# Memory attention with two gated layers on one core: the first layer's output products taken over pairs of batches, and the order around them rewritten

## Chip, core and metric

The kernel runs on one core of one Trainium2 chip. The metric is the device time of one execution in microseconds (us), the median of several runs.

## What is computed

The reference, cut to what matters. Batch 4, heads 8, sequence 576, head size 64, 32 memory slots; 2304 tokens of 512, hidden size 1536:

```python
a    = softmax(phi over the sequence)            # per batch, head and memory slot
k_m  = einsum('bhsm,bhsd->bhmd', a, k)
v_m  = einsum('bhsm,bhsd->bhmd', a, v)
attn = softmax(q @ k_m.T / 8) @ v_m              # over the 32 memory slots
x    = attn as 2304 x 512
x    = ((x @ w_a) * (x @ w_b)) @ w_out           # first layer
out  = (silu(x @ w_gate) * (x @ w_val)) @ w_out2 # second layer
```

The weights arrive as 8-byte floats and are decoded on the core to 4-byte ones.

## The kernel before

The program has two parts.

**The planned part** holds the attention and the first layer. Its order is written out by hand as a table (`PLAN`, L608 to L671 before): a row of names, each of which advances one generator by one step. Every engine runs its instructions in exactly the order in which the table issues them, and the DMA issues of SP stand in that order too. A second table, `STEPS`, says for some operations on which engine (A = ACT, V = DVE, P = POOL) they run.

The names that matter here. `p` (`att_phi`, L267) is the softmax of phi and the k_m, v_m products of one batch ("kv" products, 72 small ones), `q` transposes q, `s` makes the scores, `o` transposes the attention weights, `c` decodes a chunk of a weight, `W` loads one, `P K L Q` load phi, k and v, q. `z` (`warm`, L588) is a dummy product of the identity with itself, 256 columns wide, whose result nobody reads.

The first layer works transposed, and since x is attention weights times v_m, its input products go through v_m @ w. For a step f (128 of the 1536 hidden columns) and a batch b:

- `v` (`vw_part`, L472) makes v_m @ w for one step, for two batches from step 2 on: 8 products of 32 rows by 256 columns per batch ("vw" in the profile). ACT copies the high part (`vwh`, L500), DVE makes the low part (`vwl`, L502).
- `a` and `b` (`s1_a`, `s1_b`, L515 and L519) are the two input products of 12 matmuls each, 288 columns wide. After `b`, ACT copies it to `bs` (L523), DVE multiplies by `a` (L525), ACT makes the high part `gh` (L529) and DVE or POOL the low part `gl` (L531).
- `d` (`s2_part`, L537) is the output product of one batch, one of four 128-column blocks `dt` of the output, and two steps: two halves of 288 columns with 6 matmuls each, high and low parts crossed. It is added to `acc` by DVE (L570), or copied there for the first two steps (L568). With the last two steps, ACT and DVE split the sum into `xh` and `xl` (L580, L582), the input of the second layer.

All PE results go through four PSUM buffers (`bank2`). `g` tiles come from a pool of four, each for one batch and one step.

**The second part** (L714 on) is the second layer: units of `gate` and `val` products (24 matmuls of 384 columns, L738), their activation, and output products of 512 columns. A scheduler places it, behind the planned part on every engine.

Of the kernel before, what the change touches and what calls it, by code (L numbers as in the profile page):

```python
# [18 lines left out]
def kernel(  # L19
# [452 lines left out]
    def vw_part(parts):  # L472


        pv = bank2("vw").rearrange("c g (n x) -> c g n x", n=2)
        for n, (f, b) in enumerate(parts):
            for j in range(PR):
                for g in range(2):
                    rows = slice(D * g, D * g + D)
                    nc.tensor.matmul(  # L480
                        pv[M * j:M * j + M, g, n],
                        lhsT=vt[b][rows, M * j:M * j + M],
                        rhs=whl[f][0][rows, j].rearrange("p t c -> p (t c)"),
                        start=True,
                        stop=True,
                        tile_position=(D * g, M * j),
                    )
        yield
        f, b = parts[0]
        if f > 1 or b not in vw_2:  # L490
            vw_2[b] = [
                vw_p.tile([128, 2, 2, 256], FP32R, tag=f"vw{x}", name=f"vw{x}") for x in "hl"
            ]
        t = vw_2[b]
        o = int(f == 1)
        for n, (f, b) in enumerate(parts):
            vw_t[b, f] = [x[:, o + n] for x in t]
        n = len(parts)
        hi, lo = [x[:, o:o + n].rearrange("c n g x -> c g n x") for x in t]
        nc.scalar.copy(out=hi, in_=pv[:, :, 0:n])  # L500
# [36 lines left out]
    def s2_part(b, idx, dt):  # L537
        first, last = idx[0] == 0, idx[-1] == NF - 1
        if first and b not in acc:
            acc[b] = slot(f"acc{b}", [128, KD, 2, HB], FP32)  # L540
        if last:
            j = b // 2
# [5 lines left out]
            if dt not in x2[j][1]:  # L548
                x2[j][1][dt] = ph_p.tile(
                    [128, 2 * S], FP32R, tag=("phi", "sc")[dt // 2], name=f"xl{dt}"  # L550
                )
# [1 line left out]
        cs = slice(dt * 128, (dt + 1) * 128)
        for hb in range(2):
            terms = []
            for i in idx:
                gh, gl = g_t[b, i]
                oh, ol = ohl[i]
                terms += [
                    (oh[:, cs], gh[:, hb]),  # L560
                    (oh[:, cs], gl[:, hb]),
                    (ol[:, cs], gh[:, hb]),
                ]
            products(p[:, hb, 0:HB], terms)
# [2 lines left out]
        if first:
            copy(eng("acc", KD * b + dt), acc[b][:, dt], pv)  # L568
        else:
            nc.vector.tensor_tensor(  # L570
                out=acc[b][:, dt], in0=pv, in1=acc[b][:, dt], op=ALU.add
            )
        if last:
            yield
            cs = slice(b % 2 * S, (b % 2 + 1) * S)
            hi, lo = [
                x[:, cs].rearrange("p (h s) -> p h s", h=2)
                for x in (x2[j][0][:, dt], x2[j][1][dt])
            ]
# [2 lines left out]
            nc.vector.tensor_tensor(out=lo, in0=acc[b][:, dt], in1=f32(hi), op=ALU.subtract)  # L582

    vws = [((f, b),) for b in range(B) for f in range(2)] + [
        ((f + o, 2 * p), (f + o, 2 * p + 1))
        for f in range(2, NF, 2) for p in range(2) for o in range(2)
    ]
# [26 lines left out]
    c4 W8 c5 b0.0 p2 v1 v3 p2 c5 W9 c4 s1.0 b0.0 v3 v1 c4 p2 v1 s1.1 s1.0 b0.0 c13 s1.0 c13 b0.1
    L3 s1.1 s1.0 e2 s1.1 a0.1 s1.0 b0.1 s1.1 s1.1 p2 c13 b0.1 b0.1 b0.1 c7 p2 q2.1 p2 c7 c7
    d0.0.0 p2 q2.1 p2 d0.1.0 p3 d0.0.0 s1.1 s1.0 p3 p2 d0.1.0 c13 d0.3.0 p2 p3 s1.1 p2 s1.0 p3
    d0.3.0 d0.2.0 p3 c13 p3 o1.1 c7 W10 o1.0 q2.0 d0.2.0 e3 o1.1 p3 q2.0 o1.1 o1.0 c7 o1.0 c10
    p3 q2.2 W18 v5 p3 c10 c10 p3 c10 a1.1 q2.2 v5 p3 c10 v5 s2.1 c10 W14 p3 c10 s2.1 s2.0 p3
    s2.1 p3 s2.1 a1.0 s2.0 Q3 s2.1 s2.0 b1.1 s2.1 s2.0 s2.1 s2.0 b1.0 b1.1 b1.1 s2.0 v4 b1.1
# [233 lines left out]
```

## Time and profile before

| what | before |
|---|---|
| median of 3 runs | 868.36 us (867.11 to 868.68) |
| the profiled execution's own time | 867.69 us |
| span from first to last instruction | 865.9 us |
| PE busy | 839.0 us, 97% |
| DVE, ACT, POOL busy | 57%, 36%, 28% |
| mean granted clock of PE | 0.997 |

The profile is of one execution; 1.79 us of its time lie outside the span. PE is the matmul engine; its matmuls are pipelined, so that one lasts longer than the distance to the next one, and costs are read from the distance. In a profile L459 (tile `s`) is the line of all output products of both layers, L467 of the first layer's input products, L480 of vw, L591 of the dummies.

### The profile page before, as it was taken

How to read it: one execution, taken by the hardware profiler on the slowest of the kernel's cores; microseconds unless marked ns; L12 is line 12 of the kernel's file. 1: busy time of each engine (PE TensorE's matmuls, PEld its weight loads, DVE VectorE, ACT ScalarE, POOL GpSimd, SP SyncE). 2: the span in 40 equal slices, each digit the busy share in tenths (PEclk: the TensorE clock that was granted, in tenths of full speed). 3: DMA queues.
4: the chain of work that ended last, by engine and by line, in shares of the span. 5: the costliest groups of instructions: out<-in, count | busy, mean ns of one | idle time of the engine just before them, and what ended most of it. 6: DMA issues, size and time to landing. Idle time of an engine off the chain costs nothing.

```text
span 865.9 us, 15099 instructions
## 1 busy us (share of the span) xinstructions
PE 839.0 (97%) x6526; PEld 785.6 (91%) x6526; DVE 491.5 (57%) x671; ACT 315.2 (36%) x491; POOL 245.1 (28%) x183
## 2 busy tenths in 40 slices
PE   4798999999999999999999999999999999999997
PEld 3587999999999999999998999999889999998996
DVE  4887855757467577488554145535645453644334
ACT  3565746425344353265345333214212321410110
POOL 3662543435144153143133013204302220410000
PEclk9999999999999999999999999999999999999999
DMA  9974131302003012011211103102110200000015
GB/s 326 380 251 128 51 98 30 118 25 78 22 25 123 25 50 74 2 50 50 74 48 53 46 1 98 49 1 73 40 34 14 84 25 1 1 1 1 1 49 170
DMA packets 42434, 59.95 MB, mean 69 GB/s; under 512 B 4224, under 2 KB 30848, under 8 KB 42368
## 3 DMA queue, kind: packets, MB, share of 16 engines
q1 hardware_dynamic: 40928, 56.63, 20.3%
q10 hardware_dynamic: 1440, 2.36, 0.8%
q8 instruction: 51, 0.84, 0.4%
q14 instruction: 15, 0.12, 0.0%
HBM read 54.26 MB, written 4.72 MB: 68 GB/s over the span
## 4 chain that ended last, share of the span: by engine, by line
PE 91%; DVE 3%; DMA 2%; issue 1%; SPq 1%; ACT 1%; POOL 1%; POOLq 0%; DVEq 0%; ACTq 0%
PE s L459 34%; PE gate L738 17%; PE val L738 17%; PE s1a L467 9%; PE s1b L467 9%; PE vw L480 2%; DMA phi<-in_phi_dram 2%; PE sc L381 1%; PE warm L591 1%; DVE dec_a L173 1%; PE kv L303 1%; PE sc L391 0%; DVE dec_a L177 0%; DVE rm L263 0%; POOL dec_a L169 0%
## 5 line engine op out<-in xcount | busy, mean ns | idle before, releaser
L459 PE MATMUL s<-oh,g 128*128 128x512 f32 x432 | 137.0, 390 | 0.0
L459 PE MATMUL s<-gh,oh 128*128 128x288 f32 x384 | 114.9, 299 | 0.0
L459 PE MATMUL s<-gh,ol 128*128 128x288 f32 x384 | 113.2, 295 | 0.0
L459 PE MATMUL s<-gl,oh 128*128 128x288 f32 x384 | 113.1, 295 | 0.0
L189 POOL TENSOR_TENSOR dec_a<-dec_a,raw 128x512 int32<-128x512 int32 x48 | 65.7, 1369 | 119.2 <-DVE dec_a L177 53.0
L459 PEld LDWEIGHTS s<-oh,g 128*128 128x128 f32 x432 | 81.1, 188 | 16.4
L204 POOL TENSOR_TENSOR wl<-dec_a,wh 128x512 fp32r<-128x512 f32 x24 | 30.8, 1301 | 210.3 <-ACT wh L202 210.3
L459 PE MATMUL s<-ol,g 128*128 128x512 f32 x216 | 84.4, 391 | 0.0
L753 DVE TENSOR_TENSOR sg<-val,sg 128x768 f32<-128x768 f32 x36 | 34.5, 958 | 84.2 <-PE val L738 83.9
L750 DVE TENSOR_TENSOR sg<-gate,sg 128x768 f32<-128x768 f32 x36 | 34.4, 956 | 73.4 <-ACT sg L749 73.2
L783 DVE TENSOR_TENSOR oacc<-s,oacc 128x1024 f32<-128x1024 f32 (+1 forms) x50 | 55.8, 1115 | 35.6 <-PE s L459 34.7
L459 PEld LDWEIGHTS s<-gh,oh 128*128 128x128 f32 x384 | 72.2, 188 | 3.9 <-ACT bs L523 0.8
L738 PE MATMUL gate<-d_2x,wh 128*128 128x384 f32 x288 | 73.2, 335 | 0.0
L738 PE MATMUL gate<-d_2x,wl 128*128 128x384 f32 x288 | 73.2, 334 | 0.0
L738 PE MATMUL val<-d_2x,wl 128*128 128x384 f32 x288 | 73.2, 334 | 0.0
L738 PE MATMUL val<-d_2x,wh 128*128 128x384 f32 x288 | 73.1, 334 | 0.0
L459 PEld LDWEIGHTS s<-gh,ol 128*128 128x128 f32 x384 | 72.1, 188 | 0.0
L459 PEld LDWEIGHTS s<-gl,oh 128*128 128x128 f32 x384 | 72.0, 188 | 0.0
L165 ACT ACTIVATE raw<-raw 128x512 int32<-128x512 uint32 x72 | 48.0, 676 | 65.5 <-DMA raw<-in_moe_w_out_dram 48.6
L112 DVE TENSOR_TENSOR g<-sg,g 128x768 fp32r<-128x768 f32 (+1 forms) x48 | 45.2, 956 | 39.5 <-ACT g L111 39.5
L111 ACT CAST g<-sg 128x768 fp32r<-128x768 f32 (+1 forms) x48 | 31.0, 670 | 92.9 <-DVE sg L753 92.9
L177 DVE SCALAR_TENSOR_TENSOR dec_a<-raw,dec_a 128x512 int32<-128x512 int32 x72 | 56.4, 784 | 1.7
(131 smaller groups left out, 1753.9 us busy)
## 6 DMA issues: line engine op xcount, KB each, us to landing
raw<-in_moe_w_out_dram SPq DMA_DIRECT2D x24, 512.0 KB, 3.3
raw<-in_moe_w_b_dram SPq DMA_DIRECT2D x12, 512.0 KB, 4.4
raw<-in_moe_w_a_dram SPq DMA_DIRECT2D x12, 512.0 KB, 4.1
raw<-in_moe_w_val_dram SPq DMA_DIRECT2D x12, 512.0 KB, 3.5
raw<-in_moe_w_gate_dram SPq DMA_DIRECT2D x12, 512.0 KB, 4.1
d_0x<-in_k_dram SPq DMA_DIRECT2D x5, 576.0 KB, 10.3
d_0x<-in_v_dram SPq DMA_DIRECT2D x5, 576.0 KB, 10.7
phi<-in_phi_dram SPq DMA_DIRECT2D x4, 576.0 KB, 10.9
```

The source lines that it names most:

```text
L111: nc.scalar.copy(out=hi, in_=src)
L112: (eng or nc.vector).tensor_tensor(out=lo, in0=src, in1=f32(hi), op=ALU.subtract)
L165: nc.scalar.activation(out=lo, in_=lo.bitcast(U32), func=ACTF.Copy, scale=2.0 ** -29)
L177: nc.vector.scalar_tensor_tensor(out=a, in0=hi, scalar=-0x40000000, in1=a, op0=ALU.bitwise_and, op1=ALU.bitwise_or)
L189: nc.gpsimd.tensor_tensor(out=a, in0=a, in1=lo, op=ALU.add)
L204: nc.gpsimd.tensor_tensor(out=dst[1], in0=src, in1=f32(dst[0]), op=ALU.subtract)
L459: nc.tensor.matmul(dst, lhsT=l, rhs=r, start=(i == 0), stop=(i == n - 1))
L467: nc.tensor.matmul(p[:, hb, 0:HB], l, x, start=(i == 0), stop=(i == n - 1))
L738: nc.tensor.matmul(p[:, h, 0:CH], l[:, kt, o], r[:, c0:c0 + CH], start=(n == 0), stop=(n == 3 * KD - 1),)
L750: nc.vector.tensor_tensor(out=t, in0=pg, in1=t, op=ALU.mult)
L753: nc.vector.tensor_tensor(out=t, in0=pv, in1=t, op=ALU.mult)
L783: nc.vector.tensor_tensor(out=dst, in0=p[:, 0:n], in1=dst, op=ALU.add)
```

## The change

- Output products of the first layer from step 2 on run over a **pair of batches** (`f`, new `s2_part(j, n, f)`): g tiles are shared by two batches (1152 columns; the pool has two of them in place of four half as wide), and a unit is 384 columns of the pair for two of the four blocks `dt`, 12 matmuls. Steps 0 and 1 keep the old form (`s2_first`, 288 columns). `acc` of batches 0 and 1 is one tile; batches 2 and 3 use the tiles acc2 and acc3 by `dt`.
- `v` makes two steps for two batches **in one row** (two PSUM buffers, 32 small products).
- The table is new: the units of a kind stand together, the 13 dummies at its end are gone, and 15 stand in its first part where 4 stood.
- DVE, ACT and POOL steps are dealt out anew in `STEPS`; k and v of batch 0 are loaded ahead of the first weight chunk.

```diff
-    g_p = p1.enter_context(tc.tile_pool(name="g", bufs=4))
+    g_p = p1.enter_context(tc.tile_pool(name="g", bufs=2))
...
     def vw_part(parts):
-        pv = bank2("vw").rearrange("c g (n x) -> c g n x", n=2)
-        for n, (f, b) in enumerate(parts):
+        pvs = []
+        for part in parts:
+            pv = bank2("vw").rearrange("c g (n x) -> c g n x", n=2)
+            for n, (f, b) in enumerate(part):
...
+            pvs.append(pv)
         yield
+        for part, pv in zip(parts, pvs):
...
+            nc.scalar.copy(out=hi, in_=pv[:, :, 0:n])
+            yield
+            nc.vector.tensor_tensor(out=lo, in0=pv[:, :, 0:n], in1=f32(hi), op=ALU.subtract)
+            yield
...
+    def of_batch(x, n):
+        return x[:, n % 2 * S:(n % 2 + 1) * S].rearrange("p (h s) -> p h s", h=2)
...
-        g = [g_p.tile([128, 2, HB], FP32R, tag=f"g{x}", name=f"g{x}") for x in "hl"]
+        n, half = (b, f) if f < 2 else ((b // 2, f), b)
+        if n not in g_t:
+            g_t[n] = [g_p.tile([128, 2 * S], FP32R, tag=f"g{x}", name=f"g{x}") for x in "hl"]
+        g = [of_batch(x, half) for x in g_t[n]]
...
+    def s2_first(b, dt):
+        p = bank2("s2")
+        gs = [[of_batch(x, f) for x in g_t[b]] for f in range(2)]
+        products_halves(p, s2_terms(gs, range(2), dt))
+        yield
+        copy(eng("acc", KD * b + dt), of_batch(acc_of(b // 2, dt)[:, dt % 2], b), p[:, :, 0:HB])
+
+    def s2_part(j, n, f):
+        last = f + 2 == NF
+        cs = slice(n // 2 * CH, (n // 2 + 1) * CH)
+        dts = n % 2 * 2, n % 2 * 2 + 1
...
+        p = bank2("s2")
+        gs = [[x[:, cs] for x in g_t[j, i]] for i in (f, f + 1)]
+        for o, dt in enumerate(dts):
+            products(p[:, o, 0:CH], s2_terms(gs, (f, f + 1), dt))
+        yield
+        a = acc_of(j, dts[0])[:, :, cs]
+        nc.vector.tensor_tensor(out=a, in0=p[:, :, 0:CH], in1=a, op=ALU.add)
+        if last:
+            yield
+            nc.scalar.copy(out=x2[j][0][:, dts[0]:dts[0] + 2, cs], in_=a)
+            yield
+            for o, dt in enumerate(dts):
+                nc.vector.tensor_tensor(
+                    out=x2[j][1][dt][:, cs], in0=a[:, o], in1=f32(x2[j][0][:, dt, cs]),
+                    op=ALU.subtract,
+                )
...
     PLAN = """
-    P0 W1 K0 L0 W0 Q0 p0 P1 c1 W3 p0 c1 c1 p0 p0 K1 p0 c1 p0 c1 L1 e0 p0 c0 W2 c0 c0 c0 p0 c0 z0
...
-    d2.2.10 c39 d2.3.10 d3.2.10 c39 d3.2.10 d3.0.10 d2.3.10 d3.2.10 d2.3.10 z4 d3.3.10 z5
-    d3.0.10 z6 z7 d3.1.10 d3.0.10 z8 d2.3.10 z9 z10 d3.0.10 z11 z12 z13 z14 z15 z16
+    P0 L0 K0 W1 W0 Q0 p0 P1 W3 p0 p0 p0 K1 z0 p0 p0 z1 e0 L1 p0 c1 c1 c1 c1 c0 W2 c0 c0 c1 c0 p0
...
+    f1.5.10 f1.3.10 f1.5.10 f1.2.10 f1.2.10 f1.4.10 f1.3.10 f1.2.10 f1.3.10 f1.3.10
+    f1.4.10 f1.4.10 f1.4.10
```

Three places in PE's order. **The border between the two parts**, on PE. Before, the last unit of `d` is followed by the dummies and then by the second layer's first `gate`:

```order
L459 MATMUL s_4927<-gl,oh 128x288
L459 MATMUL s_4927<-gh,ol 128x288
L591 MATMUL warm<-ident 128x256 x13
L738 MATMUL gate<-d_2x,wh 128x384 x2
L738 MATMUL gate<-xl_4525,wh 128x384 x2
L738 MATMUL gate<-d_2x,wl 128x384 x2
```

With the change the last `f` unit (batches 2 and 3) stands directly ahead of the same `gate`:

```order
L459 MATMUL s_4624<-gl,oh 128x384
L459 MATMUL s_4624<-gh,ol 128x384
L762 MATMUL gate<-d_2x,wh 128x384 x2
L762 MATMUL gate<-xl_4295,wh 128x384 x2
L762 MATMUL gate<-d_2x,wl 128x384 x2
```

The dummies went; from `gate` on, PE's order of units is the same in both kernels.

**Ahead of an output product in the middle**, on PE. Before, v_m @ w of one step (two batches, vt_98 and vt_99) stands between other units:

```order
L459 MATMUL s_3257<-gl,oh 128x288
L459 MATMUL s_3257<-gh,ol 128x288
L480 MATMUL vw<-w,vt_98 32x256 x8
L480 MATMUL vw<-w,vt_99 32x256 x8
L459 MATMUL s_3293<-gh,oh 128x288
```

With the change two steps follow each other (four rows of vw), ahead of a unit of 384 columns:

```order
L467 MATMUL s1a<-d_1x,vwl 128x288 x2
L482 MATMUL vw<-w,vt_98 32x256 x8
L482 MATMUL vw<-w,vt_99 32x256 x8
L482 MATMUL vw<-w,vt_98 32x256 x8
L482 MATMUL vw<-w,vt_99 32x256 x8
L459 MATMUL s_1981<-gh,oh 128x384
```

Such rows of vw number 18 before from step 2 on (16 of one step, 2 of two) and 10 now; for steps 0 and 1 they are 7 before and 5 now.

**Behind the second batch's kv products**, in the start, on PE. Before:

```order
L363 MATMUL qT<-ident,d_0x 128x128 x8
L428 MATMUL aT<-ident,sc 128x128 x5
L338 MATMUL kvT<-ident,kvm 128x128 x3
L428 MATMUL aT<-ident,sc 128x128 x4
L363 MATMUL qT<-ident,d_0x 128x128 x8
L480 MATMUL vw<-w,vt_97 32x256 x8
L467 MATMUL s1a<-d_1x,vwh 128x288 x4
```

With the change:

```order
L619 MATMUL warm<-ident 128x256
L363 MATMUL qT<-ident,d_0x 128x128 x8
L428 MATMUL aT<-ident,sc 128x128 x5
L619 MATMUL warm<-ident 128x256
L338 MATMUL kvT<-ident,kvm 128x128 x3
L428 MATMUL aT<-ident,sc 128x128 x4
L363 MATMUL qT<-ident,d_0x 128x128 x2
L619 MATMUL warm<-ident 128x256 x2
L482 MATMUL vw<-w,vt_96 32x256 x8
L482 MATMUL vw<-w,vt_97 32x256 x16
L467 MATMUL s1b<-d_1x,vwh 128x288 x4
```

Dummies came in between, three rows of vw stand together, and the larger part of q's transposes (x8) moved behind.

## Rows read from the trace of the kernel before

**Rows 1.** The page: busy time, and the span in 40 slices.
```profile
PE 839.0 (97%) x6526; PEld 785.6 (91%) x6526; DVE 491.5 (57%) x671; ACT 315.2 (36%) x491; POOL 245.1 (28%) x183
...
PE   4798999999999999999999999999999999999997
```

**Rows 2.** Windows: us; busy of PE, PEld, DVE, ACT, POOL; granted clock; DMA share, GB/s.
```profile
0.00:22.00 22.00, 10.76 (x178) 8.55 (x178) 9.51 (x24) 8.40 (x13) 8.11 (x13) 1.00 0.96 327
22.00:90.00 68.00, 58.30 (x1051) 48.33 (x1052) 56.48 (x102) 40.91 (x75) 34.03 (x27) 0.97 0.70 240
90.00:412.72 322.72, 322.06 (x2925) 307.37 (x2923) 214.88 (x293) 145.38 (x227) 123.91 (x84) 1.00 0.17 55
412.72:866.00 453.28, 447.87 (x2377) 421.37 (x2375) 210.62 (x255) 120.56 (x179) 79.08 (x60) 1.00 0.14 41
```

**Rows 3.** The chain that ended last, in order of time: start us, us, what.
```profile
394.36 12.75 PE s L459 x96
407.11 5.61 PE warm L591 x26
412.72 4.18 PE gate L738 x24
...
458.51 5.48 PE s L459 x24
```

**Rows 4.** The chain between 200 and 232 us: rows of one and of two steps.
```profile
202.84 1.02 PE vw L480 x32
...
226.41 1.89 PE vw L480 x64
```

**Rows 5.** PE around one row of vw, in order of time.
```profile
381.68 0.29 PE L459 MATMUL s<-gh,ol 128*128 128x288 f32 x1
381.91 1.09 PE L480 MATMUL vw<-w,vt 64*32 64x256 f32 x32
```

**Rows 6.** From an s1a product to its g, by engine, in order of time.
```profile
384.34 0.43 PE L467 MATMUL s1a<-aT,vwl 128*128 128x288 f32 x2
...
384.81 0.76 DVE L525 TENSOR_TENSOR bs<-s1a,bs 128x576 f32<-128x576 f32 x1 [0.55 <-PE s1a L467]
...
385.61 0.68 ACT L529 CAST gh<-bs 128x576 fp32r<-128x576 f32 x1
...
386.36 1.43 POOL L531 TENSOR_TENSOR gl<-bs,gh 128x576 fp32r<-128x576 f32 x1 [0.29 <-ACT gh L529]
```

**Rows 7.** What PE waited for from 90 to 412 us: total, times, longest us.
```profile
PE s1b L467 <- DVE vwl L502: 0.7, 1, 0.7
```

**Rows 8.** DVE writing the last low parts of batches 0 and 1.
```profile
389.74 2.53 DVE L582 TENSOR_TENSOR xl<-d_0x,d_2x 128x576 fp32r<-128x576 f32 x2
```

**Rows 9.** Groups by line: the wide product of DVE with a PSUM operand.
```profile
L753 DVE TENSOR_TENSOR sg<-val,sg 128x768 f32<-128x768 f32 x36 | 34.5, 958 | 84.2 <-PE val L738 83.9
```

**Rows 10.** What PE waited for from 22 to 90 us (first of 12).
```profile
PE kv L303 <- issue: 2.8, 2, 1.8
```

**Rows 11.** Marks in PE's order in the start.
```profile
22.34 0.30 PE L275 MATMUL mx<-ident,pm 128*128 128x128 f32 x1 [0.80 <-DVE pm L265]
...
32.21 1.07 PE L363 MATMUL qT<-ident,d_0x 128*128 128x128 f32 x8 [0.51 <-DMA d_0x<-in_q_dram]
...
53.77 0.31 PE L303 MATMUL kv<-kv,phi 64*32 64x128 f32 x4
...
72.09 0.42 PE L363 MATMUL qT<-ident,q 128*128 128x128 f32 x2
```

**Rows 12.** The chain: half a score unit.
```profile
47.05 0.62 PE sc L381 x16
47.67 0.23 PE sc L391 x4
```

**Rows 13.** Windows of two stretches, columns as in rows 2.
```profile
69.00:72.00 3.00, 1.16 (x62) 0.69 (x45) 2.18 (x5) 1.60 (x3) 0.00 (x0) 1.00 0.59 175
73.00:76.50 3.50, 3.50 (x26) 3.19 (x20) 2.09 (x5) 1.72 (x5) 1.50 (x2) 0.51 0.00 0
```

More of the change, by code (lines that the diff above doesn't have):

```diff
@@ L443 @@
     STEPS = """
-    gl PPPVVPVVVPVPVPPPPPPVPVVPVVPPPVVVVVVVVVPVVVPPPVVP rmx VVVV mul PVVPVPVP sub VVVVVVVV sum
-    PPPV qT AAAVAAAAAVAA acc AAAAAAVAVVAAAAAA clamp VPVPVPPPVVVPVPPVPPVVVPVVVVVPPVVPVVPPPVPVPV
+    gl VPPVVPPPVVVPPVVVVVPPVVPVPVVVPVPPVVPVPPVVVPVPPPVV rmx VVVV mul PVPVPPPV sub VVVVVVVV sum
+    VPPV qT AAAVAVVAAAVV acc VVVAVAVAAVVVVVVA clamp VVVVVPVPPVVVPPPVVPVVPPVVVVVVVVVVPVVPVVPVVV
     """
@@ L472, in vw_part @@
     def vw_part(parts):
-        pv = bank2("vw").rearrange("c g (n x) -> c g n x", n=2)
-        for n, (f, b) in enumerate(parts):
[L477 to L487, printed above, removed]
@@ L488, in vw_part @@
-        yield
[L489 to L500, printed above, removed]
@@ L501, in vw_part @@
-        yield
-        nc.vector.tensor_tensor(out=lo, in0=pv[:, :, 0:n], in1=f32(hi), op=ALU.subtract)
+        pvs = []
+        for part in parts:
+            pv = bank2("vw").rearrange("c g (n x) -> c g n x", n=2)
+            for n, (f, b) in enumerate(part):
+                for j in range(PR):
+                    for g in range(2):
+                        rows = slice(D * g, D * g + D)
+                        nc.tensor.matmul(
+                            pv[M * j:M * j + M, g, n],
+                            lhsT=vt[b][rows, M * j:M * j + M],
+                            rhs=whl[f][0][rows, j].rearrange("p t c -> p (t c)"),
+                            start=True,
+                            stop=True,
+                            tile_position=(D * g, M * j),
+                        )
+            pvs.append(pv)
@@ new lines, in vw_part @@
+        yield
+        for part, pv in zip(parts, pvs):
+            f, b = part[0]
+            if f > 1 or b not in vw_2:
+                vw_2[b] = [
+                    vw_p.tile([128, 2, 2, 256], FP32R, tag=f"vw{x}", name=f"vw{x}") for x in "hl"
+                ]
+            t = vw_2[b]
+            o = int(f == 1)
+            for n, (f, b) in enumerate(part):
+                vw_t[b, f] = [x[:, o + n] for x in t]
+            n = len(part)
+            hi, lo = [x[:, o:o + n].rearrange("c n g x -> c g n x") for x in t]
+            nc.scalar.copy(out=hi, in_=pv[:, :, 0:n])
+            yield
+            nc.vector.tensor_tensor(out=lo, in0=pv[:, :, 0:n], in1=f32(hi), op=ALU.subtract)
+            yield
@@ L531, in s1_b, with acc_of, s2_terms @@
         eng("gl", B * f + b).tensor_tensor(out=g[1], in0=bs, in1=f32(g[0]), op=ALU.subtract)
-        g_t[b, f] = g
         yield
     acc, x2 = {}, {}
[L537 to L540, printed above, removed]
+    def acc_of(j, dt):
+        if j not in acc:
+            if j:
+                x = [slot(f"acc{b}", [128, 2, 2 * S], FP32) for b in (2, 3)]
+            else:
+                t = slot("acc0", [128, KD, 2 * S], FP32)
+                x = t[:, 0:2], t[:, 2:4]
+            acc[j] = x
+        return acc[j][dt // 2]
+    def s2_terms(gs, idx, dt):
+        terms = []
+        cs = slice(dt * 128, (dt + 1) * 128)
+        for (gh, gl), i in zip(gs, idx):
+            oh, ol = ohl[i]
+            terms += [(oh[:, cs], gh), (oh[:, cs], gl), (ol[:, cs], gh)]
+        return terms
+    def s2_first(b, dt):
[3 more added lines that the diff above has]
+        yield
+        copy(
+            eng("acc", KD * b + dt),
+            of_batch(acc_of(b // 2, dt)[:, dt % 2], b), p[:, :, 0:HB],
+        )
+    def s2_part(j, n, f):
+        last = f + 2 == NF
+        cs = slice(n // 2 * CH, (n // 2 + 1) * CH)
+        dts = n % 2 * 2, n % 2 * 2 + 1
         if last:
-            j = b // 2
             if j not in x2:
@@ L547, in s2_part @@
                     x2[j][1] = {kt: t[:, kt] for kt in range(KD)}
[L548 to L551, printed above, removed]
-        p = bank2("s2")
[L553 to L564, printed above, removed]
@@ L565, in s2_part @@
-        pv = p[:, :, 0:HB]
-        yield
[L567 to L572, printed above, removed]
+            for dt in dts:
+                if dt not in x2[j][1]:
+                    x2[j][1][dt] = ph_p.tile(
+                        [128, 2 * S], FP32R, tag=("phi", "sc")[dt // 2], name=f"xl{dt}"
+                    )
+        p = bank2("s2")
@@ L580, in s2_part @@
-            nc.scalar.copy(out=hi, in_=acc[b][:, dt])
-            yield
[L582 to L586, printed above, removed]
+            nc.scalar.copy(out=x2[j][0][:, dts[0]:dts[0] + 2, cs], in_=a)
+            yield
+            for o, dt in enumerate(dts):
+                nc.vector.tensor_tensor(
+                    out=x2[j][1][dt][:, cs], in0=a[:, o], in1=f32(x2[j][0][:, dt, cs]),
+                    op=ALU.subtract,
+                )
@@ L587 @@
+    vws = [(((f, b),),) for b in range(B) for f in range(2)] + [
+        tuple(((f + o, 2 * p), (f + o, 2 * p + 1)) for o in range(2))
+        for f in range(2, NF, 2) for p in range(2)
     ]
@@ L614 @@
[L614 to L619, printed above, removed]
@@ new lines @@
+    q2.0 c13 c10 p3 d0.0.0 q2.1 c10 p3 d0.1.0 c13 q2.1 p3 p2 d0.3.0 d0.1.0 c10 p2 c10 p2 s1.1
+    d0.3.0 p2 c10 p2 s1.1 L3 z12 p2 d0.2.0 s1.0 p2 s1.1 W7 c10 s1.0 s1.1 v5 d0.2.0 c10 v4 s1.1
+    v5 q2.2 v5 z13 v4 s1.1 q2.2 z14 v4 s2.1 s1.1 c13 o1.0 p3 s2.1 o1.0 c13 s2.1 o1.0 W9 s2.1 e3
+    o1.1 s2.0 o1.1 o1.1 p3 s2.1 Q3 a1.0 p3 s2.1 p3 s2.0 s2.1 p3 b1.1 s2.0 c26 s2.0 c26 p3 b1.1
+    a1.1 p3 s2.0 c26 p3 b1.0 b1.1 W8 s2.0 b1.1 s2.0 q3.2 q3.0 b1.0 q3.2 b1.0 v7 q3.0 b1.1 o2.1
+    v7 q3.1 o2.1 v7 s3.0 b1.0 o2.1 c7 b1.0 q3.1 c7 o2.0 s3.0 v6 c7 o2.0 s3.0 s3.1 v6 o2.0 c8
@@ new lines @@
+    s3.0 v6 b2.1 c8 c8 s3.1 c9 s3.0 c9 a2.1 s3.1 b2.1 s3.0 s3.1 c8 a2.0 b2.1 s3.0 s3.1 b2.1
+    d1.2.0 s3.1 c7 d1.0.0 d1.2.0 b2.1 s3.1 d1.1.0 d1.0.0 c8 o3.1 c9 W11 d1.1.0 o3.0 c7 o3.1 b2.0
+    o3.0 o3.1 W24 o3.0 d1.3.0 c9 b2.0 c11 b2.0 c9 b3.1 d1.3.0 c11 c11 W6 b2.0 c11 b3.0 b3.1 b2.0
+    a3.1 b3.0 c11 d2.3.0 c6 b3.1 W14 c11 b3.1 c11 d2.2.0 d2.3.0 c6 c6 b3.1 d2.0.0 d2.2.0 c6
+    d2.1.0 d2.0.0 c6 a3.0 d2.1.0 W12 b3.0 v8 b3.0 b3.0 d3.3.0 v8 c12 v8 d3.2.0 v8 d3.3.0 v8 c12
+    c12 d3.0.0 d3.2.0 b0.3 d3.0.0 c12 a0.3 b0.3 c12 b1.3 b0.3 W17 b0.3 b0.2 b0.3 b1.3 a1.3 b0.2
@@ new lines @@
+    d3.1.0 b1.3 b1.3 b1.2 b1.3 c17 d3.1.0 c17 c17 a1.2 b1.2 c17 a0.2 b1.2 c17 b1.2 b0.2 v9 c17
+    W28 b1.2 b0.2 c17 f0.4.2 b0.2 v9 c24 v9 v9 f0.2.2 f0.4.2 c24 c28 v9 c14 b3.2 c28 c24 f0.2.2
+    c14 c14 b2.3 b3.2 c24 b3.3 b2.3 c28 c14 f0.0.2 b3.3 c28 c24 f0.1.2 f0.0.2 c28 W15 c25 c25
+    f0.5.2 c25 c28 W16 f0.1.2 c14 c25 W21 f0.3.2 c15 f0.5.2 c28 c15 b2.2 c15 f0.3.2 c25 a3.3 c15
+    W37 c15 a3.2 b3.3 b3.3 W20 a2.3 b3.3 b3.2 b2.2 b3.2 a2.2 b2.3 b3.2 b2.3 b2.2 v10 b2.3 b2.2
+    b2.2 f1.4.2 v10 v10 v10 f1.1.2 f1.4.2 v10 f1.2.2 f1.1.2 b1.5 f1.2.2 f1.5.2 b1.5 f1.0.2
@@ new lines @@
+    f1.5.4 f1.1.4 v13 v13 v13 f1.2.4 f1.1.4 v13 f1.0.4 f1.2.4 b3.7 f1.0.4 b2.7 b3.7 f1.3.4 b2.7
+    b3.6 f1.3.4 c22 c22 c22 c22 a2.6 b3.6 c22 a3.7 c22 W27 a3.6 c22 b3.7 b3.7 a2.7 b3.7 b3.6
+    b3.6 c27 b2.6 b3.6 c27 b2.7 c27 b2.7 f1.5.6 c27 b2.6 b2.6 b2.7 f1.4.6 b2.6 f1.5.6 c27 b2.6
+    v12 W29 f1.4.6 f1.3.6 v12 c36 v12 c29 f1.1.6 v12 f1.3.6 c29 c29 v12 c36 b1.6 c37 f1.1.6 c37
+    c29 b0.7 b1.6 c36 c37 f1.2.6 b0.7 c36 c37 f1.0.6 f1.2.6 c29 c36 c29 W34 b1.7 f1.0.6 c29 c36
+    W31 a1.7 b1.7 c36 a0.7 b1.7 c37 b1.7 b0.6 c37 W33 b1.7 b0.7 c37 b0.7 a0.6 b0.6 b0.7 a1.6
@@ new lines @@
+    W42 b2.9 b3.9 b3.8 c35 b2.9 c35 b3.8 a3.9 c35 b3.9 f1.1.8 b3.9 b3.8 b3.9 c35 f1.0.8 f1.1.8
+    c35 b3.9 v16 c35 W41 f1.0.8 c35 f1.4.8 v16 v16 v16 f1.3.8 f1.4.8 v16 b0.10 f1.3.8 f1.2.8
+    b0.10 f1.5.8 f1.2.8 b0.11 f1.5.8 c41 c41 c41 c41 a0.10 b0.11 c41 a1.11 b0.10 c41 W40 b0.10
+    a0.11 c41 b0.10 a1.10 b0.11 b0.11 b1.11 c40 b0.11 c40 b1.10 c40 b1.11 c40 f0.1.10 b1.11
+    b1.10 c40 b1.10 b1.11 b1.11 c40 W43 v17 b1.10 f0.1.10 b1.10 f0.1.10 f0.0.10 f0.1.10 v17 c40
+    c39 v17 v17 f0.2.10 f0.0.10 c39 c38 c39 v17 f0.0.10 f0.5.10 c38 c38 f0.2.10 f0.2.10 b2.10
@@ L675, in work @@
             "c": lambda n: chunk(order[n]), "v": lambda n: vw_part(vws[n]),
-            "d": lambda b, dt, f: s2_part(b, (f, f + 1), dt),
+            "d": lambda b, dt, f: s2_first(b, dt), "f": s2_part,
         }.get(w, lambda *n: load(w, *n))(*n)
```

78 lines of the change are left out of this document (23 added, 55 removed), and 2 rows, old and new, of the table WHERE.

## The prediction
> **What bounds the kernel now.** I began with the page's busy times and slices [rows 1]: PE is busy 97% of the span and nine tenths or more of every slice but the first three and the last, while DVE stands at 57% and ACT and POOL lower. Such an average hides stages, so I cut the span in windows [rows 2]. From 90.00 to 412.72, the first layer, PE is busy 322.06 of 322.72 us; in the second layer it stays fed but for its tail. Only ahead of 90 us does it stand: 11.24 of the first 22 us and 9.70 of the next 68. So in the first layer time is gained by taking products or pauses out of PE's own row, and in the start by an order that lets it wait less. The chain in order of time [rows 3] gives prices from start to start, which a busy time cannot, since PE's matmuls overlap: 12.75/96 = 132.8 ns for 288 columns, 4.16 to 4.18/24 = some 174 ns for 384 columns, 5.48/24 = 228 ns for 512. The second layer's code and PE's order in it are the same in both kernels, so I expect its 453 us unchanged and look at the planned part alone.
>
> **Columns.** The change replaces 960 products of 288 columns (80 units of 12) by 720 of 384 (60 units); both are 276,480 columns. From 384 to 512 columns a product grows by (228.3 - 174.2)/128 = 0.423 ns a column, which leaves 132.8 - 288 x 0.423 = 11 ns that each product costs whatever its width. 240 fewer products save 240 x 11 = 2.7 us, all on PE's path. The additions of DVE fall from 80 to 60, each a third wider; a width of 768 takes 0.96 us [rows 9], and a unit on PE takes 12 x 0.174 = 2.09 us, so DVE keeps up: I cost them at nothing, covered by the next unit.
>
> A rule speaks against a term of this size. The Trainium skill ("TensorE: Matmul & The Clock Gate", section "Wait — 56ns, not 53.3ns?") gives a fixed cost of some 2.5 ns a matmul at full clock; by that, an estimate, 240 x 2.5 = 0.6 us would be saved and the sum below would be 2.1 us smaller. The rows show three widths on one line with 11 ns over, and I take the rows.
>
> **v_m @ w in one row.** A row of one step takes 1.02 us of the chain, a row of two 1.89 [rows 4], so joining saves 2 x 1.02 - 1.89 = 0.15. Around a row there is more: the product ahead of it starts 0.23 us before it [rows 5], where two products stand 0.13 apart, 0.10 over, and that falls away once per join. From step 2 on rows go from 18 to 10: 8 x 0.25 = 2.0 us.
>
> **Dummies at the end.** 26 records (13 products in two passes each) take 5.61 us on the chain between the last output product and the first gate [rows 3], 0.432 us for a dummy. Do they cover a wait? The first gate and val need x of batches 0 and 1 alone, and DVE wrote the last low part of these from 389.74 to 392.27 [rows 8], 15 us before the dummies begin. What is late next is x of batches 2 and 3, which the second pair of gate and val needs, two units or 8.3 us later. In the new order the six last units belong to these batches, and the columns that are wanted first come first. Each needs from DVE an addition of 0.96 and two differences of half the width, some 2 us against 2.09 of PE, so DVE ends about 3 us behind and is covered by 8.3. I take all 5.6 us; the bounds are 0 (the wait appears in their place) and 5.6.
>
> **The start.** 11 dummies more stand here: 4.75 us if none of them falls into a wait, which is the bound on the bad side. On the good side stand 9.70 us of idle PE from 22 to 90 [rows 2], the largest item 2.8 us at the kv products with nothing shown that was waited for [rows 10], and a half clock: from 73.00 to 76.50 the granted clock is 0.51, after a stretch in which PE was busy 1.16 of 3.00 us [rows 13], which costs about 3.5 x 0.5 = 1.75 us. Between these ends I follow the new order along its marks [rows 11]. The second batch's mx at 22.34 and its q at 32.21 wait for DMAs that stand in SP's order behind the same loads as before: no gain. From 32.21 to the third batch's kv products, 53.77 before, the change has one score unit less (twice 0.85, or 1.7 us [rows 12]), 0.5 less for joined vw, and five dummies (2.2 us) more: equal content, some 15.3 us, so 6.3 us of what lies between the marks are waits now. In the new order I find 2.7 of them left: some 1.6 until POOL has decoded the second weight for the first row of vw, and 0.8 until DVE has the third batch's maximum. That puts the third kv products at 50.2. From there to the end of the fourth, 72.09 before, stand 19.4 us of products, three dummies among them, and 1.3 of waiting for the third batch's q: 70.9, or 72.7 if PE again stands 1.8 us inside the kv products. By that mark the change has done one score unit and two rows of vw more and four transposes less, 2.5 us. So it is 1.9 to 3.7 us ahead; with half a chance that the spell of half clock goes, I take 3.0.
>
> **New waits in the first layer.** Before, PE waits once in it, 0.7 us [rows 7]. The g tiles now hold two batches, and the two of a kind serve one group (a pair of batches, a pair of steps); there are 10 groups. No g of the next group can be written until the last of six units has read the old tile. The order answers that: the first finished pair of products, whose g would be written, comes behind the group's last unit. The other way round, a unit needs g of products just made: from the end of an s1a product, 384.77, to the end of gl, 387.79, are 3.0 us [rows 6], and the new order leaves at least two units of s1 (2 x 1.6 = 3.2 us) or a row of vw and more between them. gl is wanted only by the second matmul. That is covered, barely in three or four of the ten; behind the waiting unit stands all of PE. I add 1.0 us (10 x 0.1), with 0 and 4 as bounds. The two PSUM buffers of a joined row are free after two copies of ACT and two differences of DVE, while two units (4.2 us) run: covered.
>
> **The sum.** -2.7 - 2.0 - 5.6 - 3.0 + 1.0 = -12.3 us. Against the profiled execution's own time, 867.69 us, that is 855.4; it lies 0.67 below the median of the runs, so against that I say 856.0.
>
> **Rivals.**
> 1. The start gives nothing: the dummies fall where PE would have had work, or new stalls take the place of the old. Speaking for it, loads bound the first 60 us and the largest wait shows no cause. Then the term runs from 0 to +4.75: 859.0 to 863.8.
> 2. The fixed cost of a product is small, as in the rule above, or the 384 column products pay more between two PSUM halves: without the 2.7 us, 858.1 to 858.7.
> 3. The dummies were a cover: with nothing at the border PE waits there for x or for a buffer, and then goes on at the lower clock as after 72 us [rows 13]. The 5.6 are not gained, 861.6, or 863.4 with 1.8 for the clock. Against it stands the end of the low parts at 392.27 [rows 8]. The Trainium skill ("TensorE: Matmul & The Clock Gate", section "Why this matters for your kernels") tells to leave no idle gaps between bursts of matmuls since the clock falls; by that rule a row of dummies at a border has a use, and the trace agrees that the clock falls, once, in the start.
> 4. Slower: the group change stops PE. If a unit's g comes later than its cover at each of 10 changes, because ACT and DVE have decoding in their rows ahead of it, every change costs that much. It decides from (12.3 + 1.0)/10 = 1.3 us a change on; with the whole chain of 3.0 uncovered it is 30 us, less the gains 13.3: 885. Against it: ACT and DVE are busy 45% and 67% of the first layer's window [rows 2], and the order separates products and readers.
>
> **How the numbers follow.** The forecast case (852 to 858.5) has 0.67, rival 1 0.14, rival 2 0.05, rival 3 0.09, rival 4 0.05. The range 850.5 to 862.0 leaves out the farther half of rivals 1 and 3, all of 4, and the case that the start gains most of its 9.70. A measurement of this kernel can tell 0.2%, 1.7 us, from no change. Rivals 1 to 3 are all faster by more than that unless two of them meet; rival 4 holds most of the other side. So faster 0.93, same 0.03, slower 0.04.
>
> **What would show it.** In the profile after: output products of 384 columns at 173 to 175 ns from start to start; vw as x64 in the chain at 1.89; no warm ahead of the first gate and no idle PE there; the first gate near 400 (412.72 - 12.3); from 90 us to the first gate PE idle under 2 us in all; the third batch's kv products near 50 and the fourth's end near 71. Wrong would be: waits of units on gh or gl, or of s1 on vwl, that sum to over 4 us; a gate that waits; more idle than 9.70 in the start; a second layer other than 453 us.

## The result and the profile after

The changed kernel takes 858.29 us where the kernel before took 867.74 beside it (medians): a ratio of 0.9897, interval 0.988 to 0.9914. One of its four runs, the profiled one, was a disturbed execution of 2899 us; the other three took 857.71 to 858.36, and the profile after is that of the first experiment, where the changed kernel ran again unaltered: 858.1 us with a span of 856.0. There it took 858.43 against 866.66, 0.99 (0.9883 to 0.9917). So the change gains 8.2 to 9.5 us. The forecast was 856.0 with a range of 850.5 to 862.0: the sign and the range held, and the gain came out 3 to 4 us smaller than the 12.3 of the sum.

Its page, the row of busy times that answers to [rows 1]:

```profile
PE 831.8 (97%) x6282; PEld 782.1 (91%) x6282; DVE 502.3 (59%) x681; ACT 308.3 (36%) x476; POOL 226.1 (26%) x172
```

Its windows, with the columns of [rows 2], and below them two stretches of the start:

```profile
0.00:22.00 22.00, 11.73 (x185) 9.01 (x185) 12.52 (x29) 8.76 (x15) 3.33 (x8) 1.00 0.97 329
22.00:90.00 68.00, 61.18 (x1080) 51.70 (x1082) 58.04 (x107) 37.76 (x68) 30.74 (x26) 0.97 0.70 239
90.00:402.58 312.58, 310.92 (x2650) 299.92 (x2645) 217.08 (x282) 136.72 (x210) 112.82 (x79) 1.00 0.18 57
402.58:856.00 453.42, 448.00 (x2377) 421.46 (x2376) 214.62 (x266) 125.04 (x186) 79.17 (x60) 1.00 0.13 41
32.34:55.05 22.71, 18.03 (x182) 15.05 (x182) 19.89 (x32) 12.38 (x22) 10.13 (x7) 0.92 1.04 364
48.00:51.50 3.50, 3.50 (x18) 2.90 (x17) 1.79 (x4) 1.19 (x2) 0.96 (x1) 0.54 1.10 351
```

The second layer is what it was (453.3 us), so everything lies ahead of the first gate. The chain of waits in order of time (start, length, what) shows a row of vw and the border:

```profile
143.95 1.89 PE vw L482 x64
...
390.25 12.49 PE s L459 x72
402.74 4.16 PE gate L762 x24
```

The border is closed: 72 products at 12.49/72 = 173.5 ns, then the gate, with no dummy and no wait. It stands at 402.74 where it stood at 412.72 [rows 3]: 10.0 us earlier (the two profiled executions differ by 9.6, 867.69 and 858.1). What PE waited for (total, times, longest), first from 90 us to the gate, then between the second batch's q and the third batch's kv products:

```profile
PE aT L428 <- DVE sc L417: 1.7, 1, 1.7
...
PE qT L363 <- ACT vt L347: 2.1, 1, 2.1
PE mx L275 <- DVE pm L265: 1.8, 1, 1.8
PE aT L428 <- DVE sc L417: 0.8, 1, 0.8
PE qT L363 <- DMA d_0x<-in_q_dram: 0.5, 1, 0.5
```

The first of the third batch's kv products and the last of the fourth's:

```profile
55.05 0.31 PE L303 MATMUL kv<-kv,phi 64*32 64x128 f32 x4
76.03 0.30 PE L303 MATMUL kv<-d_0x,phi 64*32 64x128 f32 x4
```

In the first layer not one wait is on `gh`, `gl` or `vwl`. The only one, 1.7 us, belongs to the attention: nine transposes of batch 3's weights at 103 us wait for a division on DVE.

From the idle of PE the start can be settled. From 0 to 22 us it fell from 11.24 to 10.27 us, from 22 to 90 from 9.70 to 6.82: 3.85 less. Eleven dummies more took 4.75, and the wait at 103 us is new, 1.66. Both profiles have one spell of half clock (73.00 to 76.50 before, 48.00 to 51.50 now, granted 0.51 and 0.54, the 1.2 GHz level). So the start is 4.75 - 3.85 + 1.66 = 2.6 us longer, 0.9 of it ahead of 90 us, where the sum had it 3.0 shorter. The sign that the prediction had set for a lost start, more than 9.70 us of idle, does not show it: idle fell to 6.82 while dummies filled PE's row.

### The profile page after: what moved, and what is told of

It is laid out like the page before. It is cut to its first block, busy times and chain, and to the rows that moved or that the text cites. A ratio compares the mean times of both kernels' runs of the same rounds, so it can differ in the third digit from the quotient of the medians.

```text
span 2897.3 us, 14574 instructions
## 1 busy us (share of the span) xinstructions
PE 2885.4 (100%) x6282; PEld 2025.0 (70%) x6282; DVE 490.5 (17%) x681; ACT 308.7 (11%) x476; POOL 222.0 (8%) x172
## 4 chain that ended last, share of the span: by engine, by line
PE 100%; DMA 0%; DVE 0%; issue 0%
PE s L459 34%; PE val L762 18%; PE gate L762 18%; PE s1b L467 9%; PE s1a L467 9%; PE s L467 3%; PE vw L482 3%; PE kv L303 1%; PE qT L363 1%; PE sc L381 1%; PE warm L619 1%; PE aT L428 1%; PE sc L391 0%; PE kvT L338 0%; DMA phi<-in_phi_dram 0%; PE mx L284 0%
## 5 line engine op out<-in xcount | busy, mean ns | idle before, releaser
L459 PE MATMUL s<-oh,g 128*128 128x512 f32 x432 | 418.4, 1091 | 0.0
L459 PE MATMUL s<-ol,g 128*128 128x512 f32 x216 | 237.4, 1099 | 0.0
L762 PE MATMUL gate<-d_2x,wl 128*128 128x384 f32 x288 | 217.0, 891 | 0.0
L762 PE MATMUL val<-d_2x,wh 128*128 128x384 f32 x288 | 216.9, 890 | 0.0
L762 PE MATMUL val<-d_2x,wl 128*128 128x384 f32 x288 | 216.7, 890 | 0.0
L459 PE MATMUL s<-gh,ol 128*128 128x384 f32 x240 | 212.3, 884 | 0.0
L459 PE MATMUL s<-gl,oh 128*128 128x384 f32 x240 | 211.9, 883 | 0.0
L459 PE MATMUL s<-gh,oh 128*128 128x384 f32 x240 | 211.5, 881 | 0.0
L467 PE MATMUL s1b<-d_1x,vwh 128*128 128x288 f32 x288 | 152.1, 735 | 0.0
L467 PE MATMUL s1a<-d_1x,vwh 128*128 128x288 f32 x288 | 151.7, 738 | 0.0
```

The source lines that it names most:

```text
L459: nc.tensor.matmul(dst, lhsT=l, rhs=r, start=(i == 0), stop=(i == n - 1))
L467: nc.tensor.matmul(p[:, hb, 0:HB], l, x, start=(i == 0), stop=(i == n - 1))
L762: nc.tensor.matmul(p[:, h, 0:CH], l[:, kt, o], r[:, c0:c0 + CH], start=(n == 0), stop=(n == 3 * KD - 1),)
```

## The experiments

Ten kernels ran; a ratio against before stands with its interval. The three theories on the missing 2.9 us were: the start gave nothing (A), the group changes stall PE (B), the columns saved less (C).

**1. The change itself.**

> The changed kernel as it is, for its profile. The change took 9.4 us off where the sum said 12.3, so 2.9 us are missing. Theory A (the start gave nothing): the third batch's kv products stand at 53 to 54 us and the fourth's end at 72 or later, and the first gate at 412.7 - 9.4 = 403.3 with under 2 us of waits from 90 us to it. Theory B (the group changes stall PE more than the 1.0 us put in): the start is 2 to 4 us ahead (third kv products near 50), and waits of output products on gh or gl, or of input products on vwl, sum to about 4 us between 90 us and the first gate. Theory C (the columns saved less): start and waits as in the sum, and products of 384 columns stand over 177 ns apart.

The profile shown above. A holds and goes further: the third kv products begin at 55.05 and the fourth's end after 76 us, both later than before (53.77 and 72.09), and the gate stands at 402.74. B falls: no wait on g or vwl. C falls: 173.5 ns.

**2. The dummies at the end alone.** The table of before, without its last 13 dummies:

```diff
-    ... d2.3.10 z4 d3.3.10 z5
-    d3.0.10 z6 z7 d3.1.10 d3.0.10 z8 d2.3.10 z9 z10 d3.0.10 z11 z12 z13 z14 z15 z16
+    ... d2.3.10 d3.3.10
+    d3.0.10 d3.1.10 d3.0.10 d2.3.10 d3.0.10
```

> The kernel before with its 13 last dummies left out and nothing else changed. If they covered nothing, as the sum has it: 5.6 us less than before (ratio 0.9935), the first gate near 407.1 and no wait of PE ahead of it. If they were a cover for x of batches 2 and 3, or for a PSUM buffer: between 0 and 5.6 us less, with a wait at the first or third gate; if PE's clock falls at that wait, 0 to 2 us more than before.

861.17 against 866.66: 0.9937 (0.9921 to 0.9953), 5.5 us. Its chain has no wait at the border:

```profile
393.25 12.75 PE s L459 x96
406.00 4.16 PE gate L746 x24
```

They covered nothing. Rival 3 falls, and this term of the sum stands to 0.1.

**3. The columns alone.** The change with units of 288 columns, 8 a group (the two more stand in the table, and DVE's additions are as narrow):

```diff
-        cs = slice(n // 2 * CH, (n // 2 + 1) * CH)
+        cs = slice(n // 2 * HB, (n // 2 + 1) * HB)
...
-            products(p[:, o, 0:CH], s2_terms(gs, (f, f + 1), dt))
+            products(p[:, o, 0:HB], s2_terms(gs, (f, f + 1), dt))
...
```

> The changed kernel with its output products of steps 2 to 11 at 288 columns instead of 384: 8 units a group in place of 6, the two added ones ahead of the group's last. 240 products more, the same columns. With 11 ns for each product whatever its width: 2.7 us more than the change (ratio 1.0031). With the 2.5 ns of the Trainium skill (TensorE: Matmul & The Clock Gate, Wait - 56ns, not 53.3ns?), an estimate by that page: 0.6 us more. If the wider product cost as much as it saved: 0.

860.9 against 858.43 of the change (ranges 860.55 to 861.03 and 858.1 to 858.61): 2.5 us for 240 products, 10.3 ns each. The chain of its last units has the same spacing as before:

```profile
392.96 12.77 PE s L459 x96
```

12.77/96 = 133.0 ns against 173.5 ns for 384 columns; by these, 960 x 133.0 - 720 x 173.5 is 2.8 us. The runs' 2.5 also hold two waits of 0.4 for `vwl` that the change does not have, so 10.3 ns is not exact; but both stand near the 11 ns that the prediction read from three widths, and rival 2 falls. The 2.5 ns of the Trainium skill ("TensorE: Matmul & The Clock Gate", section "Wait — 56ns, not 53.3ns?") do not hold for these products; the measurement decides.

**4. v_m @ w split again.** The change with the second step's row one step of the table later (20 rows where 10 stood):

```diff
+        def row(part):
...
+            return pv
+        pvs = [row(parts[0])]
         yield
-        for part, pv in zip(parts, pvs):
+        for k, part in enumerate(parts):
+            if k + 1 < len(parts):
+                pvs.append(row(parts[k + 1]))
+            pv = pvs[k]
```

> The changed kernel with v_m @ w of the second step in a row of its own, one step of the table later, mostly behind one other unit: 20 rows where 10 stood. By the price of a row (0.15 of the chain and 0.10 at the product ahead of it): 10 x 0.25 = 2.5 us more than the change (ratio 1.0029). If rows cost nothing of their own, or the split lets the low parts come earlier and takes a wait away: 0 or less.

863.97 against 858.43: 5.5 us, twice what was expected; against before 0.9967 (0.9954 to 0.998). Two things had been left out. The first shows in the change itself, around one row of vw in order of time (start, length, instruction):

```profile
229.86 0.34 PE L459 MATMUL s<-gh,ol 128*128 128x384 f32 x1
230.13 1.96 PE L482 MATMUL vw<-w,vt 64*32 64x256 f32 x64
232.02 0.44 PE L459 MATMUL s<-gh,oh 128*128 128x384 f32 x1
232.30 0.34 PE L459 MATMUL s<-gl,oh 128*128 128x384 f32 x1
232.47 0.34 PE L459 MATMUL s<-gh,ol 128*128 128x384 f32 x1
```

From product to product stand 0.17 us (the last two rows). The row starts 0.27 after the product ahead of it, which the prediction had counted (0.10 over). But behind the row the second product also comes 0.28 after the first, another 0.11 over. A row therefore costs 0.15 + 0.10 + 0.10 = 0.35 us, not 0.25, and ten rows 3.5. The second is a wait, at 146 us of the split kernel:

```profile
145.89 0.45 PE L459 MATMUL s<-gh,oh 128*128 128x384 f32 x1
146.45 0.44 PE L459 MATMUL s<-gl,oh 128*128 128x384 f32 x1
146.73 0.34 PE L459 MATMUL s<-gh,ol 128*128 128x384 f32 x1
```

The product with `gl` comes 0.56 after the first, twice the 0.28 of the change: gl is late. The joined row of 1.89 us, ahead of a group's first unit, was its cover; with 1.02 in its place three of the ten group changes wait, 0.19 to 0.29 us at gl and 0.1 at the product behind it, and an output unit of the old form at 122.9 us, that also stood behind a joined row, waits 0.9 for `gh` and `gl`: 1.9 us in all. With the 3.5 that is 5.4 of the 5.5.

**5 and 6. The dummies of the start**, all 15 away, and the last five alone:

```diff
-    ... K1 z0 p0 p0 z1 e0 ... z2 z3 Q1 p0 ...
+    ... K1 p0 p0 e0 ... Q1 p0 ...
```

> The changed kernel with none of its 15 dummies. Theory: ten of them stand ahead of a wait (for a load, for DVE's maximum, for a copy of ACT) and cost nothing; the five from 54 us on stand ahead of work and cost 0.43 each, 2.2 us: so 856.2 against 858.4 of the change (ratio 0.9975). Rival 1, all fall into waits: 858.4. Rival 2, they hold the clock: without them more stretches at the lower level, each of some 3.5 us costing 1.75; with two more of them than the change has, 859.7 or above.

> The changed kernel without the last five of its 15 dummies alone (those from 54 us on). Theory: the same 2.2 us as without all of them, 856.2, since the first ten lie in waits. If all 15 lie in waits: 858.4. If the first ten hold the clock up: this is faster than the kernel without any by 1.75 or more.

Without any: 859.57 (857.05 to 860.7), 0.9911 (0.9894 to 0.9928), beside 858.43; without the last five 858.88 (858.09 to 859.51). No gain in either: the theory of 2.2 us falls. Windows of the kernel without any (two rows), and of the change in the same stretches (two rows):

```profile
17.00:22.00 5.00, 2.53 (x22) 2.14 (x20) 2.72 (x9) 4.10 (x9) 1.30 (x1) 1.00 1.07 371
22.00:33.50 11.50, 11.12 (x247) 8.80 (x248) 7.78 (x12) 4.29 (x8) 4.65 (x5) 0.55 1.06 378
17.00:22.00 5.00, 3.42 (x26) 2.79 (x25) 2.68 (x9) 3.76 (x9) 1.29 (x1) 1.00 1.07 371
22.00:33.50 11.50, 9.55 (x257) 7.02 (x257) 10.37 (x21) 5.90 (x10) 5.65 (x6) 1.00 1.07 379
```

After a stretch in which PE was busy 2.53 of 5.00 us the granted clock is 0.55 for 11.5 us (most of it at 0.50, the 1.2 GHz level), up to 11.5 x 0.45 = 5.2 us lost; with the dummies PE was busy 3.42 us in that stretch and the clock was 1.00 up to 33.5. That is the mechanism of this experiment's rival 2, in one profile of each kernel. In time it is not shown: the median is 1.1 us above the change's, but two of the five runs, 857.05 and 857.45, are below all of the change's, and the first of them has a mean granted clock of 0.993, the second 0.998. The Trainium skill ("TensorE: Matmul & The Clock Gate", section "Why this matters for your kernels") advises against idle gaps between bursts of matmuls; this trace agrees, with the 0.55. And the waits of PE from 54 to 90 us for which nothing is shown, without the last five:

```profile
PE kv L303 <- issue: 1.4, 1, 1.4
PE sc L381 <- issue: 0.6, 1, 0.6
```

A third wait, 0.5, is for DVE's division. In the change the whole list holds one wait of 0.3. So the five dummies (2.2 us) left, and 2.0 us of waiting came with nothing shown that was waited for. Their leaving alone does not make it: in the profiles of experiments 3, 4, 7, 8, 9 and 10, which keep the five, the third batch's kv products wait 0.6 to 1.1 us in the same way. What PE lacks there stays open; it was not tried.

**7. More work ahead of the late division.** One s1b unit and a copy ahead of the nine transposes at 103 us:

```diff
-    ... c8 o3.1 c9 W11 d1.1.0 o3.0 c7 o3.1 b2.0 o3.0 o3.1
+    ... c8 b2.0 d1.1.0 o3.1 c9 W11 o3.0 c7 o3.1 o3.0 o3.1
```

> The changed kernel with one s1b unit and one copy of the first output products put ahead of the nine transposes of the attention weights at 103 us, where PE waited 1.7 us for DVE's division (behind two decoding steps on DVE). If the division is late by itself, 1.6 us of s1b hide it: 856.7 to 856.9. If DVE is full in that stretch, the wait comes back at the next unit that wants DVE: 858.4.

858.5, no gain. The wait came back in three pieces, 1.4 us together (PE, 90 to 402 us):

```profile
PE s L467 <- DVE d_1x L440: 0.9, 1, 0.9
PE aT L428 <- DVE d_0x L454: 0.3, 1, 0.3
PE s1b L467 <- DVE d_0x L454: 0.2, 1, 0.2
```

PE was given work, but DVE's row behind it was as late as before.

**8. The loads of before.** The first weight chunk ahead of k and v:

```diff
-    P0 L0 K0 W1 W0 Q0 p0 ...
+    P0 W1 K0 L0 W0 Q0 p0 ...
```

> The changed kernel with the first weight chunk loaded ahead of k and v of batch 0, as before. The first batch's kv products end at 15 us in the change and at 17 us before, but both then wait for the same load of q, which both queues bring at the same place: 858.4 (0), with the kv products' end back at 17. If the earlier k and v also bring ACT and DVE forward, the start loses up to 1.5 us: 859.9.

857.69 (856.75 to 858.05), 0.9896 (0.9882 to 0.9909): no loss, and if anything 0.7 less. The intervals of both ratios overlap, so a gain is not shown. The order of these loads is not what the start lost by.

**9 and 10. The division first**, alone and with the loads of experiment 8:

```diff
-    ... d1.2.0 s3.1 c7 d1.0.0 d1.2.0 b2.1 s3.1 d1.1.0
+    ... d1.2.0 s3.1 d1.0.0 d1.2.0 b2.1 s3.1 c7 d1.1.0
```

> The changed kernel with one decoding step of DVE (3.0 us in the profile of the change) put behind the copy and the division that PE's nine transposes wait for at 103 us. If the order on DVE is what makes PE wait there: the 1.7 us wait goes, 856.7 (ratio to the change 0.998), and the first gate comes 1.8 earlier, 400.8. If DVE is short of time in that stretch whatever its order: the wait comes back behind it, as when one s1b unit was put ahead: 858.4.

> The same, and the loads of the first weight chunk, k and v of batch 0 in the order of before. If the 0.7 us that this order of loads gave alone was real (its profile had no stretch at the lower clock) and the two add: 856.0 to 856.2, below both kernels. If it was within the scatter of the runs: as with the division alone.

857.28 (856.79 to 857.37), 0.9892 (0.9878 to 0.9907), and 856.97 (856.06 to 857.25), 0.9888 (0.9871 to 0.9904): 1.2 and 1.5 us below the change's 858.43, both below all of its runs, in another series whose kernel before stood at 866.51. The tenth has the lowest median; that the loads add to the division is not shown, since the two ranges overlap. DVE, then POOL, in the change, around the late division:

```profile
99.80 1.40 DVE L173 TENSOR_SCALAR dec_a<-dec_a 128x512 int32<-128x512 int32 x1
101.24 1.68 DVE L177 SCALAR_TENSOR_TENSOR dec_a<-raw,dec_a 128x512 int32<-128x512 int32 x1
102.84 0.74 DVE L454 COPY d_0x<-s 128x576 f32<-128x576 f32 x1
103.51 1.44 DVE L417 TENSOR_TENSOR sc<-sc,den 128x576 f32<-128x576 f32 x1
99.50 1.42 POOL L543 TENSOR_TENSOR gl<-bs,gh 128x576 fp32r<-128x576 f32 x1 [2.00 <-ACT gh L541]
100.87 1.49 POOL L187 TENSOR_TENSOR w<-dec_a,raw 128x512 int32<-128x512 int32 x1
```

and with the division first:

```profile
100.72 1.86 DVE L417 TENSOR_TENSOR sc<-sc,den 128x576 f32<-128x576 f32 x1
102.50 0.41 DVE L173 TENSOR_SCALAR dec_a<-dec_a 128x512 int32<-128x512 int32 x1
102.95 0.69 DVE L177 SCALAR_TENSOR_TENSOR dec_a<-raw,dec_a 128x512 int32<-128x512 int32 x1
100.65 1.31 POOL L187 TENSOR_TENSOR w<-dec_a,raw 128x512 int32<-128x512 int32 x1
103.78 1.29 POOL L187 TENSOR_TENSOR w<-dec_a,raw 128x512 int32<-128x512 int32 x1 [1.81 <-PE aT L428]
```

The division ends 2.4 us earlier, and the wait at these transposes shrinks from 1.7 to 0.7 (now for the copy behind the decoding). Of the 1.7 us expected 1.2 came. The move did two things at once: it changed the order, and the two decoding steps, 3.1 us ahead of the division, took 1.1 behind it, where POOL rested. Which of the two made the division late was not separated.

## Why the prediction held, and where it was wrong

| term | forecast, us | runs, us | from |
|---|---|---|---|
| columns | -2.7 | -2.5 (-2.8 by the spacing) | experiment 3 |
| end dummies | -5.6 | -5.5 | experiment 2 |
| vw in one row | -2.0 | -3.5 by price, -3.6 to -3.9 as the rest | rows around vw; the first gate |
| start | -3.0 | +2.6 | idle of PE and dummies |
| new waits on g and vwl | +1.0 | 0 | waits, 90 us to the gate |
| the one wait of before [rows 7] | not in the sum | -0.7 | the same |
| first gate | -12.3 | -10.0 | chain, 412.72 to 402.74 |

**The reading of the bound was right.** In the first layer PE has no room, so products and dummies taken out of its row came off the end nearly whole: columns and end dummies were forecast at 8.3 and gave 8.0. The second layer did not move.

**The step that failed is the start.** "Between these ends I follow the new order along its marks" put the third kv products at 50.2, the fourth's end at 70.9 to 72.7 and the gain at 3.0; the third stand at 55.05, the fourth end after 76 us, and the start is 2.6 longer. The step that gave way is "6.3 us of what lies between the marks are waits now" with "in the new order I find 2.7 of them left". The first number was too high already: before, PE stands 21.56 - 17.18 = 4.4 us between the marks (the row below, with the columns of [rows 2]). And with the change, from 32.34 to 55.05, the waits listed are 2.1, 1.8, 0.8 and 0.5, 5.2 in all: they did not shrink.

```profile
32.21:53.77 21.56, 17.18 (x212) 13.60 (x212) 19.56 (x30) 14.30 (x26) 14.49 (x13) 1.00 1.07 371
```

The wait for POOL's decoding, put at 1.6, is not in the list. The longest, 2.1, is for ACT's copy of `vt`, and ACT itself had waited 1.60 for a weight load a few instructions earlier. DVE's maximum took 1.8 where 0.8 was put in; here, from the change, are that wait of ACT, DVE's two steps of the maximum, the same two steps for the next batch, and POOL's rows beside the first pair:

```profile
34.07 0.69 ACT L163 ACTIVATE dec_a<-raw 128x512 f32<-128x512 f32 x1 [1.60 <-DMA raw<-in_moe_w_out_dram]
43.86 1.64 DVE L262 TENSOR_TENSOR rm<-phi 128x384 f32<-128x384 f32 x1
45.53 1.53 DVE L263 TENSOR_TENSOR rm<-rm,phi 128x384 f32<-128x384 f32 x1
54.21 0.55 DVE L262 TENSOR_TENSOR rm<-phi 128x384 f32<-128x384 f32 x1
54.79 0.56 DVE L263 TENSOR_TENSOR rm<-rm,phi 128x384 f32<-128x384 f32 x1
43.36 1.71 POOL L204 TENSOR_TENSOR ol<-dec_a,oh 128x512 fp32r<-128x512 f32 x1 [0.73 <-ACT oh L202]
45.04 1.60 POOL L189 TENSOR_TENSOR dec_a<-dec_a,raw 128x512 int32<-128x512 int32 x1
```

Beside POOL the two steps took 3.2 us; for the next batch, with POOL at rest, 1.1. The difference, 2.1, is more than the 1.8 that PE waited. I had counted PE's products between marks. But DVE was busy 19.89 of these 22.71 us, and 19.56 of 21.56 before: with another engine nine tenths full, a lighter row of PE can only make PE wait. This is argued from the rows; no run took work from DVE or ACT in that stretch. The same shows at 103 us, beyond the marks that I followed, where the new order put two decoding steps ahead of the division: 1.7 us, of which experiment 9 got 1.2 back by moving DVE's step, while experiment 7 got nothing by PE's order. Rival 1 named this mechanism ("new stalls take the place of the old") and its term of 0 to +4.75 holds the 2.6; the time it gave, 859.0 to 863.8, was not reached only because other terms were better than forecast.

**The spell of half clock was priced too high.** The prediction put 1.75 us on it with half a chance that it goes. In the change it moved from 73 to 48 us, ahead of the third kv products: 3.5 x (1 - 0.54) = 1.6. The profile of experiment 3 has the same start and no spell; there the third kv products stand 1.7 us earlier, but the transposes at 103 us only 0.3 (105.09 with the spell; one profile of each kernel):

```profile
53.36 0.31 PE L303 MATMUL kv<-kv,phi 64*32 64x128 f32 x4
104.78 1.34 PE L428 MATMUL aT<-ident,sc 128*128 128x128 f32 x9 [1.66 <-DVE sc L417]
```

Waits behind the spell took up the rest. So without it the third kv products are still 3.2 us behind the forecast mark.

**Vw was mis-sized.** The mechanism held and the row of 1.89 too, but the price of a row left out the second product behind it, 0.10, and the two rows fewer of steps 0 and 1 had been put into the start: 10 x 0.35 = 3.5 in place of 8 x 0.25 = 2.0.

**The group changes cost nothing**, so the +1.0 was a loss that did not come, and rival 4 falls. But "covered, barely in three or four of the ten" held: experiment 4 took 0.87 us of cover away, and three of the ten waited.

So the forecast was near by two errors of opposite sign: 5.6 us too good in the start, 3.2 to 3.6 too bad in vw, in the waits on g and in the old wait.

## What to carry to other kernels

Where one engine is full for hundreds of microseconds, price what leaves its row from start to start, the instructions just ahead and just behind a change of tile shape included; here columns and end dummies came within 0.2 us, and vw missed by the product that was not counted. Where several engines are nearly full, as in this start, a lighter row of one of them need not give anything: follow the fullest engine's row, and look what was put ahead of the operation that the others wait for. Dummies in front of waits cost nothing that these runs can tell, and in one profile the clock held where it fell without them; in front of a closed border 13 of them cost their full length: look at the waits behind each before counting it.

## What was not expected of the hardware

- The two decoding steps of DVE took 1.40 and 1.68 us while POOL worked beside them (99.50 to 102.36), and 0.41 and 0.69 in the pause of POOL from 101.96 to 103.78: 3.4 and 2.4 times as long beside POOL. This is no single case. From 20 to 400 us of the change, the first step took 0.41 to 0.43 us in all its 31 rows without POOL and 0.36 to 1.67 in its 9 rows beside it, five of them 1.40 or more. The Trainium skill ("Advanced Engine Details and Errata", section "VectorE Performance Modes") says that the second port of DVE is shared with POOL and that the two block each other in some modes; the rows of the first step, a TENSOR_SCALAR, agree. The second step and the two steps of the maximum stand on these rows alone.
- Leaving the last five dummies (2.2 us) out of the start did not shorten the kernel: 858.88 us beside 858.43.
